# Long convolution and routed experts on one core: the upper frequencies' products on the way out, in two row tiles and two banks

## The chip, the cores and the metric

The kernel runs on one core of a Trainium2 chip. The metric is the time of one execution in microseconds of the device; the median of three runs stands for the kernel. Engines are named as in the profile: PE is TensorE, PEld its weight loads, DVE VectorE, ACT ScalarE, POOL GpSimd, SP SyncE.

## The reference

Two stages follow each other. The first is a long causal convolution of every channel by Fourier transform; the second sends each row of the result to one of 16 experts, a two-layer network of width 1024.

```python
def _attn_ref(x, v, pos_emb, w1, w2):            # x, v: (4, 10048, 128)
    h_mlp = np.maximum(pos_emb @ w1, 0.0) @ w2
    h_filt = h_mlp * np.exp(-0.01 * np.arange(S))[:, None]
    u = x * v
    y = irfft(rfft(u, n=2*S, axis=1) * rfft(h_filt, n=2*S, axis=0)[None], n=2*S, axis=1)[:, :S]
    return x * y

def _moe_ref(x, ...):                            # x: (40192, 128)
    # group by argmax of x @ w_group, expert by argmax of xg @ w_expert[g]
    out[tok] = g_w * e_w * (np.maximum(xg @ w1[g, e], 0.0) @ w2[g, e])
```

## The kernel before

The transform over 20096 positions is split into one over 157 steps of 128 positions and one over the 128 positions inside a step. A channel of one batch is held as 79 frequencies of the outer transform. The first 64 of them (`KM`) lie in `z`, the upper 15 and a row of zeros in `zr`; each frequency has a real and an imaginary part, so that a channel fills 128 rows with its lower frequencies and 32 rows with its upper ones.

The convolution is a loop over the batches. A **pass** of batch b does two things in turns, three channels here and six there: it takes batch b in (`dft_blocks`, L393 on PE, fed by `product` L446 and `fold` L459 on DVE) and it brings batch b-1 out (`turned` and `inverse_blocks`). A **middle** stage follows each pass (`middle`, `back`): products with the filter's spectrum, frequency by frequency. There are four batches, so the way out is done four times: in three passes beside the next batch's way in, and in a last pass that has no batch to take in and that loads the first layer's weights meanwhile. Routing of a finished batch runs along on DVE, and its rows are written out to the experts' pages by indirect transfers that POOL issues (L359). After the convolution the experts' stage (`moe`) runs to the end.

The way out goes by pairs of runs, twelve channels in all (eight in the last pair of a pass). `turned` (L680, L683) transposes on PE, through three buffers of PSUM (`psT`) that ACT copies to `tt` tiles (L685): `tts[0]` holds the upper frequencies, four channels to a tile of 128 rows, and `tts[1]` to `tts[3]` the lower ones, a channel to 128 rows. Then `inverse_blocks` is called for each run of six channels. It issues the load of `x` for the run (`xo`, on ACT's queue, in the last pass on SP's, L696 and L698), takes one of two banks (`psO`, the tile `po`), and writes into it, for each of the two halves of 64 output rows, the products of the upper frequencies (L708) and those of the lower ones (L716):

```python
nc.tensor.matmul(po[hs, c - c0 : c - c0 + m], tts[0][:, g, hs],
                 self.fi[:, h, 1 + c % 4 : 1 + c % 4 + m], start=c == c0, stop=False)      # L708
nc.tensor.matmul(po[hs, c - c0], tts[1 + c // 4][:, c % 4, hs], self.fi[:, h, 0], ...)     # L716
```

A product of L708 contracts over the 128 rows of four channels. Its moving matrix `fi` is block-diagonal, 79 columns for each channel of the run among the four and zeros in the rows of the others; so it has 316 columns where the run has all four channels and 158 where it has two. L716 has 79 columns. The two halves are two column tiles of 64 on PE. ACT then folds the halves into `oo` (L725, L726), DVE adds (`yt`, L731) and multiplies by `xo` (L733); in the last pass POOL does that product for every other run.

The framework puts each instruction at a place on its engine and keeps that order; a tile that is asked for waits until the last reader of the buffer it takes is done. `psO` is also used, some times per batch, by routing's small tiles (`pl`, `pc`, `pe`).

Of the kernel before, what the change touches and what calls it, by code (L numbers as in the profile page):

```python
# [12 lines left out]
F32 = mybir.dt.float32  # L13
# [12 lines left out]
SEQ, D, NB, N1 = 10048, 128, 79, 157  # L26
KM = 64
# [3 lines left out]
NE, G, EG, FF = 16, 4, 4, 1024  # L31
# [7 lines left out]
GI = 6  # L39
# [22 lines left out]
HALVES = slice(0, 64), slice(64, 128)  # L62


def q_of_position():

    q = np.arange(128)
    return np.where(q < 64, 64 + q, 127 - q)


def p_of_position():

    q = np.arange(128)
    return np.where(q < 64, 63 - q, q)


def make_consts():
    f32 = np.float32
    k1 = np.arange(NB)
    ang = 2 * np.pi * ((k1[None, :] * k1[:, None]) % N1) / N1  # L80
    w = (np.where(k1 == 0, 1.0, 2.0) / NN)[:, None]


    fa = np.stack(
        [
            np.stack([np.cos(ang), -np.sin(ang)], 2).reshape(NB, -1),
            np.stack([-np.sin(ang), -np.cos(ang)], 2).reshape(NB, -1),
        ],
        1,
    ).reshape(NB, -1)  # L90


    fi = []
    for swap in range(2):
        both = np.zeros((KM + 16, 2, NB))
        both[:NB, swap] = w * np.cos(ang)
        both[:NB, 1 - swap] = (2 * swap - 1) * w * np.sin(ang)
        rest = np.zeros((4, 32, 4, NB))
        for i in range(4):
            rest[i, :, i] = both[KM:].reshape(32, NB)  # L100
        sign = 1 - 2 * swap
        fi += [sign * both[:KM].reshape(128, -1), sign * rest.reshape(128, -1)]
    fi = np.concatenate(fi, 1)
    k = k1[:, None] + N1 * np.arange(128)[None, :]
    s2 = 2 * np.arange(64) + 1
    a = np.pi * ((k[None] * s2[:, None, None]) % (2 * NN)) / NN
    b = np.concatenate([np.cos(a), np.sin(a)], 0)
    ph = (np.pi * ((k * 127) % (2 * NN)) / NN).T
    phase = np.stack([np.cos(ph), np.sin(ph), -np.cos(ph)], -1)
    win = np.zeros(NR * 128, f32)  # L110
    win[:SEQ] = np.exp(-0.01 * np.arange(SEQ, dtype=f32))
    win = win.reshape(NR, 128)
    return {
        "c_fa": np.concatenate([fa, np.zeros((NR - NB, 4 * NB))]),
        "c_fi": fi,
        "c_b": b,
        "c_bp": np.ascontiguousarray(b.transpose(2, 1, 0)),
        "c_phase": phase.reshape(128, NB * 3),
        "c_win": np.repeat(np.stack([win[:, 64:], win[:, 63::-1]]).transpose(0, 2, 1).reshape(2, -1), 64, 0),
        "c_tri": np.triu(np.ones((128, 128)), 1),  # L120
        "c_id": (np.arange(128)[:, None] * NB + np.arange(NB)[None, :]).astype(f32),
    }
# [10 lines left out]
def groups(n, step):  # L133
    return [(i, min(step, n - i)) for i in range(0, n, step)]


OUTS = groups(120, GI) + [(120, 4), (124, 4)]


class Kernel:  # L140
# [60 lines left out]
    def conv(self, ctx, right):  # L201
        tc, nc, d = self.tc, self.nc, self.d
# [13 lines left out]
        with ExitStack() as c2:  # L216
            self.filter(c2, ahead, made, folded)
        bp = ctx.enter_context(tc.tile_pool(name="back", bufs=1))
        self.fi = bp.tile([128, 2, 5, NB], F32, name="fi")
        nc.sync.dma_start(self.fi.rearrange("p h a t -> p (h a t)"), d["c_fi"])  # L220


# [6 lines left out]
        for b in range(self.nbat + 1):  # L229
            last = b == self.nbat  # L230
            if last:
                ahead.close()
                inner.close()
                self.sp = ctx.enter_context(tc.tile_pool(name="stream", bufs=2, reuse_waits="tile"))
                weights = self.first_weights(right)
                xy = self.z.rearrange("p k s d -> p (k s) d")[:, :NB]
            elif b > 0:
                xy = xyp.tile([128, NB, D], F32, tag="xy", name=f"xy{b - 1}")
            parts = groups(D, GD) if not last else []
            if b == 1:  # L240
                self.router_consts()
            self.run_ahead(b, 0, made, folded)
            for j, (d0, n) in enumerate(OUTS):
                if b > 0 and j % 2 == 0:
                    tts = self.turned(d0, min(2 * GI, D - d0))
                for i in range(2 * j, min(2 * j + 2, len(parts))):
                    self.run_ahead(b, i, made, folded)
                    self.scatter(1 + (i >= 12 and i % 2))
                    self.dft_blocks(*folded[i])
                    if b > 0 and i % 2 == 0:  # L250
                        self.inverse_blocks(b - 1, xy, d0, n, tts)
                if last:
                    self.inverse_blocks(b - 1, xy, d0, n, tts)
                    next(weights, None)
                    if j == 8:
                        self.scatter(sum(1 for s in self.scatters if s[0] < self.nbat - 2))
                        for p in self.all[:XG]:
                            p.load()
                for _ in range(3 if last else 1):
                    next(routing, None)  # L260
                if last:
                    self.scatter(1 + j % 2)
            made, folded = [], []
            if b > 0:
                oh = self.rp.tile([128, NE, NB], F32, tag="oh", name="oh")
                en = self.entries.tile([128, NB, 2], F32, tag="en", name="en")
                routing = chain(self.chosen(b - 1, xy, oh, en), self.ranked(b - 1, oh, en))
                if last:
                    for _ in range(CHOSEN):
                        next(routing)  # L270
            if not last:
                back = []
                for i, (k0, n) in enumerate(groups(NB, 2)):
                    back.append(self.middle(b, k0, n))
                    if len(back) > LAG:
                        self.back(*back.pop(0))
                    if b == 1 and i % 4 == 1:
                        self.clear_rest(i // 4)
                    self.scatter(i % 4 != 3)
                    if i % 4 != 3 if i < 30 else i % 2:  # L280
                        next(routing, None)
                for args in back:
                    self.back(*args)
# [402 lines left out]
            tts.append(tt)  # L686
        return tts

    def inverse_blocks(self, b, xy, d0, n, tts):

        nc, d, sp = self.nc, self.d, self.sp
        rows = lambda t: t[:, : n * NB].rearrange("p (t d) -> p t d", d=n)
# [3 lines left out]
            nc.scalar.dma_start(xo[:, : n * NB], src)  # L696
        else:
            self.tc.keep_in_program_order(nc.sync.dma_start(xo[:, : n * NB], src))  # L698
        po = self.psO.tile([128, GI, NB], F32, tag="po", name="po")
        c0 = d0 % (2 * GI)  # L700

        for c in range(c0, c0 + n):


            if c == c0 or c % 4 == 0:
                g, m = c // 4, min(4 - c % 4, c0 + n - c)
                for h, hs in enumerate(HALVES):
                    nc.tensor.matmul(  # L708
                        po[hs, c - c0 : c - c0 + m].rearrange("p c t -> p (c t)"),
                        tts[0][:, g, hs],  # L710
                        self.fi[:, h, 1 + c % 4 : 1 + c % 4 + m].rearrange("p c t -> p (c t)"),
                        start=c == c0,
                        stop=False,
                    )
            for h, hs in enumerate(HALVES):
                nc.tensor.matmul(  # L716
                    po[hs, c - c0],
                    tts[1 + c // 4][:, c % 4, hs],
                    self.fi[:, h, 0],
                    start=False,  # L720
                    stop=c == c0 + n - 1,
                )
        oo = rows(sp.tile([128, GI * NB], F32, tag="oo", name="oo"))
        by_row = po[:, :n].rearrange("p d t -> p t d")
# [4 lines left out]
        pool, tag, bufs = (self.ap, "y", NY) if b < self.nbat - 1 else (sp, "yt", 2)  # L729
# [639 lines left out]
def layout(x, v, pos_emb, w1, w2, moe_w_group, moe_w_expert, moe_w1, moe_w2):  # L1369

    nbat = x.shape[0]
    c = np.ascontiguousarray

    def blocks(a):
        p = np.zeros((nbat, NR * 128, D), np.float32)
        p[:, :SEQ] = a
        return p.reshape(nbat, NR, 128, D)

    xb, vb = blocks(x), blocks(v)
    q, p = q_of_position(), p_of_position()  # L1380
    pos = np.zeros((NR * 128, 64), np.float32)
    pos[:SEQ] = pos_emb
    pos = pos.reshape(NR, 128, 64)
# [7 lines left out]
    def twice(a):  # L1391
# [4 lines left out]
        "xv_in": c(np.stack([xb[:, :, q], vb[:, :, q]]).transpose(1, 2, 4, 0, 3)),  # L1396
        "x_out": c(
            np.concatenate(
                [xb[:, :NB, p, d0 : d0 + n].transpose(0, 2, 1, 3).reshape(nbat, 128, -1) for d0, n in OUTS], 2
            )  # L1400
        ),
        "pos_t": c(np.stack([pos[:, 64:], pos[:, 63::-1]]).transpose(0, 3, 2, 1).reshape(128, -1)),
# [2 lines left out]
        "w_router": c(  # L1405
            np.concatenate(
                [moe_w_group, moe_w_expert.transpose(1, 0, 2).reshape(128, 16), np.zeros((128, 12), np.float32)], 1
            )
        ),
        "m_w1": c(moe_w1.reshape(NE, 128, FF).transpose(1, 0, 2)),  # L1410
        "m_w2": c(
            moe_w2.reshape(NE, NC, 128, 128).transpose(2, 0, 1, 3).reshape(128, NE, FF)
        ),
# [22 lines left out]
```

## Time and profile before

| | |
|---|---|
| runs of the kernel before | 2050.03, 2047.52, 2046.69 us; median 2047.52 us |
| the profiled execution | 2044.59 us |
| its span | 2042.7 us, mean granted clock 0.977 |
| busy, share of the span | PE 95%, PEld 87%, DVE 79%, ACT 70%, POOL 65% |
| the four times that a batch is brought out | from 250.7, 453.2, 670.0 and 893.8 us on |

The span is measured from the first to the last instruction that the profiler saw; the execution's own time is 1.89 us longer. Busy shares are means over stages with different limits. The end of a matmul is modelled from its size, so PE's busy share is an upper bound; where an engine is at its limit is better read from the distance between starts. A product in 32-bit floats is recorded as two matmuls and two weight loads.

### The profile page before, as it was taken

The numbers are of one execution on the slowest core, as the hardware profiler recorded it, in microseconds if no ns is written. First come the engines' busy times: TensorE is split into PE (matmuls) and PEld (weight loads), VectorE is DVE, ScalarE is ACT, GpSimd is POOL, SyncE is SP. The second block draws the span as 40 slices with busy tenths as digits, with TensorE's granted clock in tenths as the row PEclk, the third lists the DMA queues.
The fourth block names the chain that finished last, engine by engine and source line by source line (L and its number), as shares of the span: only waits on it lengthen the run. The fifth ranks groups of instructions, "written<-read, shape, count | busy, mean of one in ns | idle before, by whom it ended". The sixth has DMA issues, their size and how long they took to land.

```text
span 2042.7 us, 52533 instructions
## 1 busy us (share of the span) xinstructions
PE 1931.5 (95%) x17166; PEld 1778.1 (87%) x17166; DVE 1604.6 (79%) x3462; ACT 1434.3 (70%) x3395; POOL 1320.1 (65%) x1371
## 2 busy tenths in 40 slices
PE   8988999979998799988899999999999999999997
PEld 8867788768876687767799999999999999999997
DVE  6687775796578765894889998889999998888885
ACT  6653387437743575446787888888888888888886
POOL 3157600675799467967176777888888885555554
PEclk9999999989999899999899999999999999999999
DMA  4699966977898588967444544555555544444442
GB/s 138 226 266 262 290 182 194 329 220 205 243 333 262 155 235 283 322 210 261 157 143 127 157 144 149 162 187 165 155 162 157 159 142 135 127 126 131 124 123 66
DMA packets 258715, 388.82 MB, mean 190 GB/s; under 512 B 32680, under 2 KB 132627, under 8 KB 258433
## 3 DMA queue, kind: packets, MB, share of 16 engines
q1 hardware_dynamic: 225024, 318.01, 51.8%
q0 software_dynamic: 23904, 51.83, 7.2%
q10 hardware_dynamic: 9504, 15.54, 2.8%
q8 instruction: 139, 2.28, 0.5%
q14 instruction: 144, 1.17, 0.2%
HBM read 303.24 MB, written 83.04 MB: 189 GB/s over the span
## 4 chain that ended last, share of the span: by engine, by line
PE 50%; POOL 2%; DVE 1%; ACT 1%; DMA 1%; issue 1%; ACTq 0%; DVEq 0%; SPq 0%; POOLq 0%
PE py L1305 8%; PE py L1303 7%; PE py L1304 7%; PE ph L1286 7%; PE ph L1284 7%; PE ph L1285 7%; PE ptm L1317 2%; PE px L1241 2%; POOL wl L1273 1%; POOL out L1329 1%; PE po L708 1%; PE po L716 1%; PE ptr L798 0%; PE pt L683 0%; DMA mw<-m_w 0%
## 5 line engine op out<-in xcount | busy, mean ns | idle before, releaser
L1293 DVE SCALAR_TENSOR_TENSOR hl<-ph,hh 128x512 fp32r<-128x512 f32 x656 | 445.2, 683 | 94.0 <-ACT hh L1292 93.4
L1292 ACT ACTIVATE hh<-ph 128x512 fp32r<-128x512 f32 x656 | 393.8, 600 | 138.7 <-PE ph L1286 70.3
L359 POOL DMA_INDIRECT prow<-stg,adr x316 | 347.1, 1098 | 126.5 <-issue 50.1
L1329 POOL DMA_INDIRECT out<-os,to x328 | 347.9, 1061 | 91.5 <-issue 71.9
L1303 PE MATMUL py<-hh,wh 128*128 128x256 f32 x1312 | 398.5, 304 | 0.0
L1284 PE MATMUL ph<-xh,wh 128*128 128x256 f32 x1312 | 373.3, 285 | 5.1 <-DVE hl L1293 2.6
L1305 PE MATMUL py<-hh,wl 128*128 128x256 f32 x1312 | 373.1, 284 | 5.3 <-POOL wl L1273 5.3
L1286 PE MATMUL ph<-xh,wl 128*128 128x256 f32 x1312 | 373.3, 285 | 0.4 <-DVE wl L1273 0.4
L1285 PE MATMUL ph<-xl,wh 128*128 128x256 f32 x1312 | 372.7, 284 | 0.0
L1304 PE MATMUL py<-hl,wh 128*128 128x256 f32 x1312 | 371.3, 283 | 0.0
L1273 POOL TENSOR_TENSOR wl<-ws,wh 128x512 fp32r<-128x512 f32 x162 | 220.1, 1359 | 201.6 <-ACT wh L1266 200.5
L1305 PEld LDWEIGHTS py<-hh,wl 128*128 128x128 f32 x1312 | 251.2, 192 | 8.2 <-POOL wl L1273 8.1
L1284 PEld LDWEIGHTS ph<-xh,wh 128*128 128x128 f32 x1312 | 252.7, 193 | 5.8 <-ACT hh L1292 2.8
L1286 PEld LDWEIGHTS ph<-xh,wl 128*128 128x128 f32 x1312 | 253.0, 193 | 0.9 <-DVE wl L1273 0.8
L1285 PEld LDWEIGHTS ph<-xl,wh 128*128 128x128 f32 x1312 | 253.0, 193 | 0.1
L1304 PEld LDWEIGHTS py<-hl,wh 128*128 128x128 f32 x1312 | 252.7, 193 | 0.0
L1303 PEld LDWEIGHTS py<-hh,wh 128*128 128x128 f32 x1312 | 251.9, 192 | 0.0
L1273 DVE TENSOR_TENSOR wl<-mw,wh 128x512 fp32r<-128x512 f32 x328 | 238.1, 726 | 0.0
L642 POOL TENSOR_TENSOR y<-t 128x256 f32<-128x256 f32 (+1 forms) x160 | 120.7, 755 | 146.0 <-DVE t L641 141.9
L1266 ACT CAST wh<-mw 128x512 fp32r x328 | 205.7, 628 | 0.0
L1266 ACT CAST wh<-ws 128x512 fp32r<-128x512 f32 x328 | 204.8, 624 | 1.3 <-DMA ws<-m_w 1.3
L393 PE MATMUL psa<-fa,eo 96*64 96x158 f32 x2048 | 182.6, 312 | 13.9 <-POOL eo L464 4.7
(237 smaller groups left out, 4198.0 us busy)
## 6 DMA issues: line engine op xcount, KB each, us to landing
ws<-m_w SPq DMA_DIRECT2D x328, 256.0 KB
ht<-hspec SPq DMA_DIRECT2D x156, 256.0 KB
xv<-xv_in SPq DMA_DIRECT2D x131, 288.0 KB
bt<-c_b SPq DMA_DIRECT2D x95, 256.0 KB
xg<-prow SPq DMA_DIRECT2D x164, 130.0 KB
bp<-c_bp SPq DMA_DIRECT2D x76, 256.0 KB
stg<-xyd SPq DMA_DIRECT2D x76, 256.0 KB
xyd<-xy SPq DMA_DIRECT2D x57, 256.0 KB
```

The lines of the kernel that those rows point to most:

```text
L359: ins = self.nc.gpsimd.indirect_dma_start(self.d["prow"], bass.IndirectOffsetOnAxis(ap=u.adr[:, t : t + 1], axis=0), u.rows[:, t - u.t0], ...
L1266: k.fix(k.nc.scalar.copy(hi, self.matrix(i, half, self.ea)))
L1273: ins = v.tensor_tensor(lo, self.matrix(i, half, self.ed), self.wh[i][half].bitcast(F32), ALU.subtract)
L1284: k.fix(nc.tensor.matmul(ph[:, j], wh, self.xh, start=True, stop=False))
L1285: k.fix(nc.tensor.matmul(ph[:, j], wh, self.xl, start=False, stop=False))
L1286: k.fix(nc.tensor.matmul(ph[:, j], wl, self.xh, start=False, stop=True))
L1292: k.fix(nc.scalar.activation(hh, ph, AF.Relu))
L1293: k.fix(nc.vector.scalar_tensor_tensor(hl, ph, 0.0, hh.bitcast(F32), ALU.max, ALU.subtract))
L1303: k.fix(nc.tensor.matmul(self.py, wh, self.hh[c], start=(c == 0), stop=False))
L1304: k.fix(nc.tensor.matmul(self.py, wh, self.hl[c], start=False, stop=False))
L1305: k.fix(nc.tensor.matmul(self.py, wl, self.hh[c], start=False, stop=(c == NC - 1)))
L1329: ins = k.nc.gpsimd.indirect_dma_start(k.d["out"], bass.IndirectOffsetOnAxis(ap=self.to[:, h : h + 1], axis=0), o[:, h], None, bounds_chec ...
```

## The change

The products of the upper frequencies are taken out of `inverse_blocks` into `inverse_rest`, which runs once for each pair of runs, ahead of the first of them, and takes both banks at once. Each set of four channels is cut into two row tiles of 64 rows, that is of two channels. A row tile's products go to a bank of their own, 158 columns each. So the first run's bank holds the first two channels of every four, the second run's the last two. The lower frequencies' products keep their size; they follow in `inverse_blocks`, which takes the bank that `inverse_rest` began. The output's channels now come in that order, and the host puts the channels of `x`, of the router's weights and of the first layer's rows in the same order. `fi` has three blocks of 79 columns for each half in place of five, and is loaded once. No load, copy or addition on another engine is added or taken away.

```diff
@@ make_consts
-        rest = np.zeros((4, 32, 4, NB))
+        rest = np.zeros((4, 32, 2, NB))
         for i in range(4):
-            rest[i, :, i] = both[KM:].reshape(32, NB)
+            rest[i, :, i % 2] = both[KM:].reshape(32, NB)
@@
+def channels():
+    order = []
+    for i, (d0, n) in enumerate(OUTS):
+        first = d0 - i % 2 * n
+        order += [first + 4 * (c // 2) + i % 2 * 2 + c % 2 for c in range(n)]
+    return np.array(order)
@@ conv
-        self.fi = bp.tile([128, 2, 5, NB], F32, name="fi")
+        self.fi = bp.tile([128, 2, 3, NB], F32, name="fi")
@@
                     if b > 0 and i % 2 == 0:
-                        self.inverse_blocks(b - 1, xy, d0, n, tts)
+                        if j % 2 == 0:
+                            pos = self.inverse_rest(min(2 * GI, D - d0), tts)
+                        self.inverse_blocks(b - 1, xy, d0, n, tts, pos[j % 2], j % 2)
                 if last:
-                    self.inverse_blocks(b - 1, xy, d0, n, tts)
+                    if j % 2 == 0:
+                        pos = self.inverse_rest(min(2 * GI, D - d0), tts)
+                    self.inverse_blocks(b - 1, xy, d0, n, tts, pos[j % 2], j % 2)
@@
-    def inverse_blocks(self, b, xy, d0, n, tts):
+    def inverse_rest(self, n, tts):
+        pos = [self.psO.tile([128, GI, NB], F32, tag="po", name="po") for _ in range(2)]
+        for g in range(n // 4):
+            for h, hs in enumerate(HALVES):
+                for po, rs in zip(pos, HALVES):
+                    self.nc.tensor.matmul(
+                        po[hs, 2 * g : 2 * g + 2].rearrange("p c t -> p (c t)"),
+                        tts[0][rs, g, hs],
+                        self.fi[rs, h, 1:3].rearrange("p c t -> p (c t)"),
+                        start=g == 0,
+                        stop=False,
+                    )
+        return pos
+
+    def inverse_blocks(self, b, xy, d0, n, tts, po, run):
@@
-        po = self.psO.tile([128, GI, NB], F32, tag="po", name="po")
-        c0 = d0 % (2 * GI)
-        for c in range(c0, c0 + n):
-            if c == c0 or c % 4 == 0:
-                g, m = c // 4, min(4 - c % 4, c0 + n - c)
-                for h, hs in enumerate(HALVES):
-                    nc.tensor.matmul(
-                        po[hs, c - c0 : c - c0 + m].rearrange("p c t -> p (c t)"),
-                        tts[0][:, g, hs],
-                        self.fi[:, h, 1 + c % 4 : 1 + c % 4 + m].rearrange("p c t -> p (c t)"),
-                        start=c == c0,
-                        stop=False,
-                    )
+        for c in range(n):
             for h, hs in enumerate(HALVES):
                 nc.tensor.matmul(
-                    po[hs, c - c0],
-                    tts[1 + c // 4][:, c % 4, hs],
+                    po[hs, c],
+                    tts[1 + c // 2][:, 2 * run + c % 2, hs],
                     self.fi[:, h, 0],
                     start=False,
-                    stop=c == c0 + n - 1,
+                    stop=c == n - 1,
                 )
@@ layout
-                [xb[:, :NB, p, d0 : d0 + n].transpose(0, 2, 1, 3).reshape(nbat, 128, -1) for d0, n in OUTS], 2
+                [xb[:, :NB, p][..., chan[d0 : d0 + n]].transpose(0, 2, 1, 3).reshape(nbat, 128, -1) for d0, n in OUTS], 2
...
-            )
+            )[chan]
-        "m_w1": c(moe_w1.reshape(NE, 128, FF).transpose(1, 0, 2)),
+        "m_w1": c(moe_w1.reshape(NE, 128, FF)[:, chan].transpose(1, 0, 2)),
```

## Rows read from the trace of the kernel before

**Rows 1.** Stretches of ten pairs each, pass by pass: length, busy by engine, clock, DMA share, GB/s.
```profile
core 0: us, PE busy (x) PEld busy (x) DVE busy (x) ACT busy (x) POOL busy (x), PEclk, DMA share, GB/s
250.70:342.40 91.70, 90.58 (x1260) 80.94 (x1260) 61.30 (x114) 75.60 (x196) 0.00 (x0) 1.00 0.65 181
453.20:555.80 102.60, 94.93 (x1266) 84.48 (x1265) 67.77 (x152) 76.71 (x196) 63.58 (x68) 0.97 0.77 218
670.00:785.90 115.90, 104.57 (x1275) 90.79 (x1275) 76.35 (x177) 77.19 (x197) 67.65 (x70) 0.89 0.70 195
893.75:957.40 63.65, 61.15 (x794) 51.54 (x794) 41.50 (x100) 41.99 (x78) 39.17 (x39) 0.97 0.86 291
```

**Rows 2.** Timeline of PE, one pair of the first pass: start, length, what.
```profile
268.52 0.55 PE L680 MATMUL pt<-ident,zr 128*128 128x128 f32 x3
...
271.06 1.02 PE L393 MATMUL psa<-fa,eo 96*64 96x158 f32 x12
271.92 0.70 PE L708 MATMUL po<-fi,tt 128*64 128x316 f32 x4
272.45 0.72 PE L716 MATMUL po<-fi,tt 128*64 128x79 f32 x16
273.00 0.44 PE L708 MATMUL po<-fi,tt 128*64 128x158 f32 x4
273.27 0.45 PE L716 MATMUL po<-fi,tt 128*64 128x79 f32 x8
273.54 1.78 PE L393 MATMUL psa<-fa,eo 96*64 96x158 f32 x24
...
276.78 0.99 PE L393 MATMUL psa<-fa,eo 96*64 96x158 f32 x12
277.70 0.55 PE L680 MATMUL pt<-ident,zr 128*128 128x128 f32 x3
```

**Rows 3.** Timeline of PE, one pair of the last pass.
```profile
951.41 0.55 PE L680 MATMUL pt<-ident,zr 128*128 128x128 f32 x3
...
954.01 0.75 PE L708 MATMUL po<-fi,tt 128*64 128x316 f32 x4
954.60 0.72 PE L716 MATMUL po<-fi,tt 128*64 128x79 f32 x16
955.14 0.45 PE L708 MATMUL po<-fi,tt 128*64 128x158 f32 x4
...
956.76 0.73 PE L716 MATMUL po<-fi,tt 128*64 128x79 f32 x16
957.42 0.44 PE L680 MATMUL pt<-ident,zr 128*128 128x128 f32 x2
```

**Rows 4.** Timeline of PE: the router's products in four column tiles of 32.
```profile
969.07 0.42 PE L806 MATMUL plt<-xrt,wr 128*32 128x128 f32 x8
```

**Rows 5.** One pair of the first and of the last pass, columns as in rows 1.
```profile
268.50:277.70 9.20, 9.16 (x129) 8.13 (x128) 6.51 (x12) 7.71 (x21) 0.00 (x0) 1.00 0.66 183
945.38:951.40 6.02, 5.92 (x82) 5.04 (x79) 2.94 (x4) 4.27 (x8) 5.23 (x7) 1.00 0.89 307
```

**Rows 6.** Waits in the second, third and last pass (453:560, 670:786, 893:962): total, times, longest.
```profile
PE pt L683 <- ACT tt L685: 7.5, 7, 1.9
...
PE pt L683 <- ACT tt L685: 7.5, 5, 2.2
...
DVE yt L731 <- POOL z L733: 6.7, 2, 3.9
```

**Rows 7.** Timeline, first pass: addition of a second run; the next pair's L708 starts at 271.92.
```profile
269.71 0.64 DVE L731 TENSOR_TENSOR yt<-po,oo 128x474 f32<-128x474 f32 x1
```

**Rows 8.** Timeline, last pass: additions of second runs, and the next pair's first product.
```profile
936.88 0.65 DVE L731 TENSOR_TENSOR yt<-po,oo 128x474 f32<-128x474 f32 x1 [3.86 <-POOL z L733]
...
941.93 0.65 DVE L731 TENSOR_TENSOR yt<-po,oo 128x474 f32<-128x474 f32 x1 [2.88 <-POOL z L733]
...
941.97 0.75 PE L708 MATMUL po<-fi,tt 128*64 128x316 f32 x4
```

**Rows 9.** The tile `fi`: its one load, and the stretch that the load falls in.
```profile
L220 SPq DMA_DIRECT2D fi<-c_fi x1: 346/346/346, 126.4 to 126.4; - x1
...
100.00:150.00 50.00, 41.89 (x357) 32.76 (x355) 41.08 (x97) 29.71 (x99) 23.95 (x35) 0.97 1.03 270
```

More of the change, by code (lines that the diff above doesn't have):

```diff
@@ L1379, in layout @@
     xb, vb = blocks(x), blocks(v)
-    q, p = q_of_position(), p_of_position()
+    q, p, chan = q_of_position(), p_of_position(), channels()
     pos = np.zeros((NR * 128, 64), np.float32)
```

## The prediction

> **What bounds the kernel now.** I first asked where the changed instructions lie. They lie only in the four passes that bring a batch out, so I read those as four stretches of ten pairs each, from one pair's first transpose to the eleventh's [rows 1]. The reader is to see two things there: PE is nearly always busy, but a pair takes 9.17 us in the first pass (91.70 / 10), 10.26 in the second, 11.59 in the third and 6.37 in the last (63.65 / 10). The first three do the same work on PE, so the first pass is near PE's own limit, and the second and third lose 1.1 and 2.4 us per pair to other things.
>
> Since the end of a matmul is modelled, I then took the timelines of single pairs and measured from start to start. A pair of the first pass runs without a visible hole: transposes, three channels in, a run out, twice three channels in, and so on, 9.18 us from 268.52 to 277.70 [rows 2]. A pair of the last pass has transposes for 2.60 us (951.41 to 954.01) and 3.41 us of products [rows 3]. In the first pass ACT is busy 7.71 us of 9.20 and DVE 6.51; in the last POOL is busy 5.23 us of 6.02 and the DMA engines 0.89 [rows 5]. These are the limits that lie next behind PE. Last I read the waits, for what the two slow passes lose: the fourth group of transposes waits for ACT's copies, 7.5 us in all in each of those two passes, and in the last pass an addition on DVE waits twice, 6.7 us, for POOL's product [rows 6].
>
> **The upper products before.** From start to start, four records of 316 columns take 272.45 - 271.92 = 0.53 us, four of 158 take 273.27 - 273.00 = 0.27 us; a pair has two of each, so 1.60 us. The lower products take 273.00 - 272.45 = 0.55 us for four channels, and 273.54 - 273.27 = 0.27 us for two [rows 2]; they stay as they are, 1.64 us per pair.
>
> **The upper products after.** Three sets of four channels, each with four products of 158 columns (two halves by two row tiles), each recorded twice: 24 records in place of 16. No row-tiled product stands in this trace, so the price is bounded from both sides. *Below:* if the four tiles run at once, a set takes what four records of 158 columns take now on two tiles, 0.27 us, and a pair 0.81 us. *Above:* if only two run at once, a set takes twice that, 0.54, and a pair 1.62 us. (That the tiles run one after the other, which would be 3.2 us, I exclude: column tiles run in pairs in every row of that kind.) The nearest row is the router's: eight records on four column tiles of 32, each 128 columns wide, are over in 0.42 us [rows 4]. If such a product takes 128/158 of the 0.27 us that a pair of 158-column products takes, that is 0.22 us for two tiles at once; two such rounds would be 0.44 us of starts and an end behind them, while the row ends within 0.42 us with the last product's end in it. So four tiles did run at once there, and each seemed to proceed on its own. I take the lower end: 0.81 us, a saving of 0.79 us per pair of twelve. The pair of eight falls from 2 x 0.53 = 1.06 to 2 x 0.27 = 0.54 us.
>
> The Trainium skill says the same of row tiles: TensorE: Matmul & The Clock Gate, Part 3, gives 3.07 times the speed for four row tiles that run together. Half of it for two, an estimate from that page, would make a pair's upper products 1.60 / 1.53 = 1.05 us, a saving of 0.55. No run here shows it yet.
>
> **The switch of tiling.** The rows of one tile change from 128 to 64 ahead of the upper products and back behind them. What a change of tiling costs can be read at the end of a pair of the last pass: the last sixteen products of L716 start at 956.76, the transposes on the whole array at 957.42, that is 0.66 us, where sixteen take 955.14 - 954.60 = 0.54 when products of the same tiling follow [rows 3]. So 0.12 us here; taking the switch from the way in to the transposes, 277.70 - 276.78 = 0.92 us where 271.92 - 271.06 = 0.86 is usual [rows 2], it would be less, so I take 0.1 us with bounds 0 (if tiles of the same columns need no pause) and 0.12. In the first three passes two switches are added per pair (from the way in, whose 64-column tiles run straight into L708 now, and to L716), in the last one (transposes end in a switch already).
>
> This is also the rule that speaks against the change: TensorEngine Tiling (Array Packing), Key Properties, has TensorE drain when the tiling mode changes. The trace agrees in the direction, by the 0.12 us above [rows 3]; without any drain the sum at PE, below, would be 7.7 us larger.
>
> **Sum at PE.** First three passes: 0.79 - 0.20 = 0.59 us per pair; with the pair of eight (0.52 - 0.20 = 0.32) 10 x 0.59 + 0.32 = 6.2 us per pass. Last pass: 10 x 0.69 + 0.42 = 7.3 us. In all 25.9 us if every pair were bound by PE alone.
>
> **What of it reaches the end.** *First pass:* a pair would fall to 8.6 us, with ACT busy 7.7 of it, in its program's order; ACT's copies free the transposes' buffers, so some of the gain becomes a wait for it. I take three quarters, 4.7 us (bounds 2 and 6.2). *Second pass:* pairs take 1.1 us more than PE needs; half, 3.1 us (0 to 6). *Third:* 2.4 us more than PE needs and a clock of 0.89 [rows 1]; a third, 2 us (-1 to 5). *Last:* POOL's 5.2 us per pair nearly fill the 5.3 us that would be left, and the DMA engines are at 0.86 [rows 1, 5]; a fifth, 1.5 us (-3 to 6), with the next point in it. What is late next is therefore ACT's copies in the first three passes, POOL's product and the loads behind it in the last.
>
> **Both banks at once.** Before, a pair's first product needed only the bank that the first run had left long ago. Now the upper products wait until the second run of the pair before has been added on DVE. Queued behind them on PE are both runs and the next way in; ACT, DVE and then POOL wait for these. In the first pass that addition ends at 269.71 + 0.64 = 270.35 and the next pair's products start at 271.92: 1.57 us to spare, the work that covers it being transposes and three channels in [rows 7]. In the last pass only transposes lie between, and where the addition has waited for POOL it ends at 942.58, after 941.97 where the products start now: 0.6 us of new wait in that pair [rows 8]. Three to five such pairs cost 2 to 3 us; it is in my figure for the last pass.
>
> **Edits at no cost.** `fi` shrinks from 3160 to 1896 bytes per partition, 0.16 MB less; its load falls in a stretch where the DMA engines are full at 270 GB/s, so at most 0.6 us [rows 9], and nothing if the load is not what the stretch waits for; I take 0. The order of channels changes no size of any load, copy or addition. The lower products of the first run now read all three `tts` of a pair, but the upper ones give ACT 0.8 us to finish the last. No transfer is issued in the moved step.
>
> **Sum.** 4.7 + 3.1 + 2.0 + 1.5 = 11.3 us. Against the profiled execution, 2044.59 us, that gives 2033.3; the median of the runs lies 2.9 us above the profiled one, so the forecast is 2047.5 - 11.3, rounded to 2036 us. The runs of before spread over 3.3 us; 0.2%, 4.1 us, is about what a measurement can tell from no change.
>
> **Rivals.**
>
> *A. The row tiles do not run at once (slower).* The place is L708's successor, the price: saving 1.60 - 1.62, about 0, and the switches remain, 3 x 11 x 0.2 + 11 x 0.1 = 7.7 us, plus 2 us of waits for the bank: 2057 us; 2050 if the switches are hidden in the passes that wait for others. For it: no row-tiled product here. Against it: column tiles do run four at once [rows 4], and the two row tiles write to different banks. It decides when a set takes over 0.47 us, since from there 0.2 us of switches eat the saving.
>
> *B. The gain goes into waits (no change).* PE's pairs get shorter, but ACT in the first pass, DVE and routing in the second and third, POOL and transfers in the last take up all but 3 us: 2044 us. For it: the two slow passes [rows 1] and the waits for ACT [rows 6]. Against it: the first pass, with PE without a hole [rows 2].
>
> *C. Waits for the second bank decide (slower).* With the tiles at once, but 1.5 us of wait in each of ten pairs of the last pass and 1 us in each of the twenty of the two slow ones: 35 us against 26, so 2057 us; it tips at a mean wait of about 0.6 us per pair. For it: rows 8 of this very wait in the making; against it: 1.57 us to spare in the first pass [rows 7].
>
> *D. PE is bound everywhere (more).* All 25.9 us arrive: 2022 us. Against it stand the waits [rows 6].
>
> **Chances.** Forecast, a gain of 5 to 22 us: 0.59. B: 0.17. A: 0.16, of which a quarter hidden well enough to be no change. C: 0.06. D: 0.02. Faster by over 0.2%: 0.59 + 0.02 = 0.61; within: 0.17 + 0.04 = 0.21; slower: 0.12 + 0.06 = 0.18. The range runs from 2025 (a gain of 22, nearly the whole sum) to 2051 (A at its mild end), which leaves out D, most of C and the harder half of A. The forecast's own range is 2025 to 2042.
>
> **What would show it.** Right: the upper products as 24 records of 158 columns on 64 rows, a set every 0.27 us, 0.8 us per pair; ten pairs of the first pass in about 87 us, and the last pass little shorter than 63.65. Wrong at the first step: a set every 0.53 us. Wrong at the switch: more than 0.12 us between the upper products and those around them. Wrong at the bank: waits of PE's upper products for DVE's addition of more than 0.5 us per pair outside the last pass. It would also be wrong if the passes got shorter and the middle stages or the experts' stage longer by as much; I see no term for that.

## The result and the profile after

The changed kernel takes 2065.98 us (median of 4 runs, 2064.99 to 2069.34) where the kernel before takes 2047.47 beside it: 1.0091 times as long, 95% interval 1.0074 to 1.0109. The forecast was 2036 us, the range 2025 to 2051. The change made the kernel 18.5 us slower; measured again (e9 below) it took 1.0069 times as long (1.0045 to 1.0093). The profiled execution took 2065.51 us, with a span of 2063.6 us.

The same stretches of ten pairs as in [rows 1], read from the windows of the kernel after, with the same columns:

```profile
252.09:352.47 100.38, 87.14 (x1342) 77.34 (x1342) 62.03 (x114) 78.35 (x196) 0.00 (x0) 0.98 0.61 164
463.18:573.41 110.23, 92.41 (x1346) 80.53 (x1346) 70.18 (x151) 79.07 (x196) 63.13 (x66) 0.92 0.72 201
691.18:803.80 112.62, 99.23 (x1356) 84.89 (x1356) 77.43 (x177) 78.11 (x197) 67.58 (x68) 0.89 0.70 200
912.36:977.09 64.73, 58.32 (x876) 50.68 (x876) 38.73 (x98) 42.13 (x78) 41.37 (x41) 0.96 0.86 289
```

PE is busy less in every pass (87.14 us against 90.58 in the first), as it was meant to be, and yet the first pass grew by 8.68 us and the second by 7.63; the third shrank by 3.28 and the last grew by 1.08. The starts and ends of these rows and of [rows 1] give what lies between: the stretches from pass to pass changed by -0.09, +3.57 and +0.71 us, the way to the first pass by +1.39 and the way from the last to the end by +1.2. The nine sum to the 20.9 us by which the spans differ (2063.6 - 2042.7). The first two passes hold 16.3 us of it, the stretch between the second and the third pass 3.6.

The timeline of PE in the first pass after, to be held against [rows 2]:

```profile
263.66 0.85 PE L696 MATMUL pt<-ident,z 128*128 128x128 f32 x4 [2.23 <-ACT tt L698]
...
265.40 1.04 PE L708 MATMUL po<-fi,tt 64*64 64x158 f32 x24
266.37 1.04 PE L729 MATMUL po<-fi,tt 128*64 128x79 f32 x24
...
273.34 0.85 PE L696 MATMUL pt<-ident,z 128*128 128x128 f32 x4 [1.04 <-ACT tt L698]
...
283.88 0.85 PE L696 MATMUL pt<-ident,z 128*128 128x128 f32 x4 [1.90 <-ACT tt L698]
```

Two things are to be seen. The upper products (L708) are 24 records on 64 rows, and from their start to that of the lower ones (L729) they take 266.37 - 265.40 = 0.97 us, where they took 1.60. But the last transposes of a pair, which used to follow the others almost at once (waits of 0.8 us in all in the whole first pass, below), now wait 1.0 to 2.2 us, in the pairs shown, for ACT's copies of the earlier ones. A pair takes 273.34 - 263.66 = 9.68 and then 283.88 - 273.34 = 10.54 us; it took 9.18.

So the question is why ACT is late. The waits of the first pass (253:342), total, times, longest; first the kernel before, then the one after:

```profile
DVE xv L446 <- DMA xv<-xv_in: 20.2, 23, 1.5
...
PE pt L683 <- ACT tt L685: 0.8, 2, 0.5
ACT xv L457 <- DVE xv L446: 0.8, 1, 0.8
```

```profile
DVE xv L459 <- DMA xv<-xv_in: 28.5, 31, 3.0
ACT xv L470 <- DVE xv L459: 17.5, 21, 1.8
...
PE pt L696 <- ACT tt L698: 11.5, 7, 2.2
```

They make a chain: DVE's product waits for a load of x, ACT's negation waits for that product (0.8 us before, 17.5 now), and ACT's copies, which PE's transposes need, stand behind the negation in ACT's queue. At its head is the load. That it is late because of the order of DVE's instructions is what the timelines suggest; the experiments below test it. In a pair DVE does four products (xv, first step of a channel group on the way in), four folds (eo, the last reader of the loaded tile, which frees its buffer for the next load), two additions (yt) and two products on the way out (xy). Timeline of DVE before, one pair (its first addition is in [rows 7]):

```profile
269.23 0.55 DVE L446 TENSOR_TENSOR xv<-xv 96x384 f32<-96x384 f32 x1 [1.15 <-DMA xv<-xv_in]
...
270.27 0.55 DVE L459 TENSOR_TENSOR eo<-xv 96x384 f32<-96x384 f32 x1
270.74 0.65 DVE L733 TENSOR_TENSOR xy<-yt,xo 128x474 f32<-128x474 f32 x1
271.40 0.55 DVE L446 TENSOR_TENSOR xv<-xv 96x384 f32<-96x384 f32 x1
272.13 0.55 DVE L459 TENSOR_TENSOR eo<-xv 96x384 f32<-96x384 f32 x1 [0.18 <-PE psa L393]
274.08 0.56 DVE L446 TENSOR_TENSOR xv<-xv 96x384 f32<-96x384 f32 x1 [1.40 <-DMA xv<-xv_in]
274.63 0.56 DVE L459 TENSOR_TENSOR eo<-xv 96x384 f32<-96x384 f32 x1
275.11 0.64 DVE L731 TENSOR_TENSOR yt<-po,oo 128x474 f32<-128x474 f32 x1
275.67 0.54 DVE L459 TENSOR_TENSOR eo<-xv 96x384 f32<-96x384 f32 x1
276.14 0.64 DVE L733 TENSOR_TENSOR xy<-yt,xo 128x474 f32<-128x474 f32 x1
276.88 0.55 DVE L446 TENSOR_TENSOR xv<-xv 96x384 f32<-96x384 f32 x1
```

And after, one whole pair and the start of the next:

```profile
269.51 0.55 DVE L459 TENSOR_TENSOR xv<-xv 96x384 f32<-96x384 f32 x1 [2.97 <-DMA xv<-xv_in]
269.98 0.64 DVE L744 TENSOR_TENSOR yt<-po,oo 128x474 f32<-128x474 f32 x1
270.55 0.55 DVE L472 TENSOR_TENSOR eo<-xv 96x384 f32<-96x384 f32 x1
271.01 0.64 DVE L746 TENSOR_TENSOR xy<-yt,xo 128x474 f32<-128x474 f32 x1
271.57 1.02 DVE L472 TENSOR_TENSOR eo<-xv 96x384 f32<-96x384 f32 x2
272.51 0.64 DVE L744 TENSOR_TENSOR yt<-po,oo 128x474 f32<-128x474 f32 x1
273.19 0.65 DVE L746 TENSOR_TENSOR xy<-yt,xo 128x474 f32<-128x474 f32 x1
274.07 0.55 DVE L459 TENSOR_TENSOR xv<-xv 96x384 f32<-96x384 f32 x1 [0.23 <-DMA xv<-xv_in]
275.19 0.55 DVE L472 TENSOR_TENSOR eo<-xv 96x384 f32<-96x384 f32 x1 [0.57 <-PE psa L406]
276.38 0.56 DVE L459 TENSOR_TENSOR xv<-xv 96x384 f32<-96x384 f32 x1 [0.63 <-DMA xv<-xv_in]
277.46 0.56 DVE L459 TENSOR_TENSOR xv<-xv 96x384 f32<-96x384 f32 x1 [0.52 <-DMA xv<-xv_in]
280.12 0.56 DVE L459 TENSOR_TENSOR xv<-xv 96x384 f32<-96x384 f32 x1 [2.11 <-DMA xv<-xv_in]
```

With P a product, F a fold, Y an addition and X a product on the way out, a pair was P Y F X P F P F Y F X P and is P Y F X F F Y X P F P P. Three folds now lie within 2.04 us (270.55 to 272.59), then comes one at 275.19 and no other up to 280.12, so three of the five load buffers come free in a bunch and their loads run together. The loads' own starts in the two traces (SP's queue) show that each is issued within 0.1 us of a fold's end: before at 270.88, 272.76, 275.22, 276.29 and 279.90 us, after at 271.15, 272.18, 272.65, 275.81 and 281.78. The DMA line of the two traces shows it (262:285, GB/s in 40 slices, before and then after):

```profile
GB/s 43 144 305 70 145 281 382 81 83 176 267 155 220 322 197 67 0 123 294 136 177 350 314 55 117 169 235 171 220 341 198 26 48 150 333 60 208 373 265 31
```

```profile
GB/s 144 192 241 123 269 139 0 30 158 343 343 259 211 13 0 14 0 112 171 246 96 150 369 279 198 301 186 298 180 264 65 10 0 0 0 0 134 315 144 171
```

Slices under 50 GB/s: five before, eleven after, and those eleven in three gaps. No line of the change puts DVE's instructions in another order; the order is worked out by the framework from the program, and moving the upper products to the head of a pair was enough for it to come out differently (ACT's too; on PE, in the first two passes, the groups other than the upper products kept their order, and only single records at their seams changed places).

### The profile page after: what moved, and what is told of

It reads as the page before. It is cut to its first block, busy times and chain, and to the rows that moved or that the text cites. A ratio compares the mean times of both kernels' runs of the same rounds, so it can differ in the third digit from the quotient of the medians.

```text
span 2063.6 us, 53237 instructions
## 1 busy us (share of the span) xinstructions
PE 1919.7 (93%) x17518; PEld 1764.7 (86%) x17518; DVE 1604.0 (78%) x3462; ACT 1441.7 (70%) x3395; POOL 1320.7 (64%) x1371
## 4 chain that ended last, share of the span: by engine, by line
PE 66%; DMA 8%; DVE 8%; POOL 5%; issue 4%; ACT 4%; SPq 1%; ACTq 0%; DVEq 0%; POOLq 0%
PE py L1318 7%; PE ph L1299 7%; PE ph L1297 7%; PE py L1316 7%; PE py L1317 7%; PE ph L1298 7%; PE psb L488 6%; DMA xv<-xv_in 5%; PE pbp L670 4%; PE psa L406 2%; PE ptm L1330 2%; PE px L1254 2%; PE ptr L811 2%; PE plt L819 1%; PE pt L696 1%
## 5 line engine op out<-in xcount | busy, mean ns | idle before, releaser
L670 PE MATMUL pbp<-y,bp 128*128 128x256 f32 x632 | 169.7, 394 | 26.2 <-POOL y L658 25.6
```

## The experiments

*Theory O (order):* regrouping the products made DVE and ACT work in another order; this starves the loads and costs more than the tiles save. *Theory B (banks):* the loss is that a pair's upper products need both banks. *Theory T (tiles):* the tiles or the switches cost more than was saved. The order is varied by pinning: each product, fold, addition and copy of the first three passes of DVE (and ACT) is held behind the one ahead of it in an order taken from the other kernel; nothing else is changed.

On the chips of the first eight and of the four runs e13 to e16 the kernel before itself took 2115 to 2119 us, so of these runs I read the ratio and the first pass, which is as long there as elsewhere. Later passes and whole times are compared among e9 to e12 (one chip), e17 and e18 (another), where before took 2048 to 2049 us; what these show of the sixth buffer does not hold on the other chips, as said below.

**e1, e16: regrouped, without row tiles** (128-row products on block-diagonal constants, as before the change).

```
...
-                        tts[0][rs, g, hs],
-                        self.fi[rs, h, 1:3].rearrange("p c t -> p (c t)"),
+                        tts[0][:, g, hs],
+                        self.fi[:, h, 1 + 2 * r : 3 + 2 * r].rearrange("p c t -> p (c t)"),
...
```

> The changed kernel with its upper products regrouped in the same way (ahead of both runs, into both banks), but each contracting over all 128 rows against a block-diagonal matrix, as before; the orders on DVE and ACT come out the same as in the changed kernel. Theory 'order' (the framework's new order of DVE's and ACT's instructions in the passes costs the time, the row tiles save some): still slow, ten pairs of the first pass 99 to 106 us, 2064 to 2082 us in all. Rival 'tiling' (the row tiles or the switches of tiling cost the time): back near the kernel before, 91 to 94 us, 2045 to 2053 us. Rival 'banks' (taking both banks at once costs the time): slow as under 'order'.

> The regrouped products over all 128 rows, for the whole time; same order as the changed kernel. 'Order': 1.006 to 1.016, first pass 99 to 102 us: the row tiles neither cost nor save where the passes wait for the loads. If the row tiles cost: 1.000 to 1.004.

Ratios 1.008 (1.0039 to 1.0122) and 1.0100 (1.0062 to 1.0138), first pass 100.7 and 99.2 us. DVE's order was that of the changed kernel. The loss is there without a single row tile, and in e16 at a granted clock of 1.00 through the first pass: T falls as its cause, and in that pass the clock is not the cause either. e16 also gives the price of the upper products when only two tiles run at once, the same 24 records on 128 rows (timeline of PE, 268:290):

```profile
273.49 1.84 PE L708 MATMUL po<-fi,tt 128*64 128x158 f32 x24
275.12 1.04 PE L729 MATMUL po<-fi,tt 128*64 128x79 f32 x24
```

From start to start that is 1.63 us, against 0.97 with row tiles.

**e2, e5, e13, e18: the changed kernel in the order of before; e4: DVE's order alone.**

```
...
+        for order in ORDERS:
+            at, last = {k: iter(v) for k, v in self.seen.items()}, None
+            for kind in order:
+                ins = next(at[kind])
+                if last is not None:
+                    self.after(ins, last)
+                last = ins
...
```

> The changed kernel, with the passes' additions, products and copies on DVE and ACT pinned to the order that they had in the kernel before. 'Order': the loss is gone and the row tiles show, ten pairs of the first pass 85 to 89 us, 2027 to 2043 us. 'Banks': no change against the changed kernel, 98 to 102 us, 2060 to 2070 us. 'Tiling': the same, 2058 to 2070 us.

> The changed kernel with the order of before on DVE and ACT, once more, since the runs beside it had spread over 40 us. 'Order' and 'loads' (the order costs the time; the row tiles save PE time, but the five load buffers hold the passes near their old length): ten pairs of the first pass 91 to 94 us, in all 2043 to 2058 us. 'Order' alone (nothing else bounds): 85 to 89 us and 2027 to 2043. If the order is not the cause: 2060 to 2070 us.

> The changed kernel with DVE alone pinned to the order of before; ACT's order is the framework's. 'Order', if DVE's bunched products and folds (and so the freeing of the load buffers) are what costs: as the run with both pinned, 85 to 90 us for ten pairs, 2027 to 2045 us. If it is ACT's order (negations ahead of the copies that PE waits for): 95 to 101 us, 2055 to 2068 us.

> The changed kernel with the order of before on DVE and ACT and its five load buffers, for the whole time, which the two earlier runs of it could not give beside a kernel before that spread over 40 us. 'Order': the loss is gone, 0.992 to 1.001 of the kernel before, first pass 91 to 95 us. If the order matters in the first pass alone: 1.000 to 1.005.

> The changed kernel with the order of before and five load buffers, likewise. 'Order' as the whole of the loss: 0.990 to 1.001 of the kernel before; 1.003 to 1.006 if the last pass and the middle stages keep a part of the loss.

Ratios 1.0029 (0.9978 to 1.0079), 1.0048 (0.9999 to 1.0098), 1.0021 (0.9982 to 1.0059) and, the closest, e18's 1.0026 (1.001 to 1.0042); first passes 92.9, 95.4, 92.7 and 94.6 us. e4: 1.0041 (0.999 to 1.0092), 93.1 us. The old order gives most of the first pass's loss back, and DVE's alone does (e4). But the 85 to 90 us that 'Order' forecast for e2 and e4 did not come, and not even in the old order is the kernel faster than before; the waits of e18 in the stretch 264:342 say why:

```profile
DVE xv L497 <- DMA xv<-xv_in: 25.6, 15, 2.9
...
PE pt L738 <- ACT tt L740: 6.9, 8, 1.6
```

DVE still waits 25.6 us for loads, where the kernel before waits 17.4 in that stretch. So O explains only part: with a shorter pair on PE, five buffers do not bring loads in time in the old order either. In the second pass e18 takes 106.7 us, where the changed kernel takes 110.2 (111.6 in e9) and the kernel before 102.6: there the old order gives back about half. The third takes 113.9 us in e18 and 114.1 in e9, so it does not depend on the order.

**e3, e6, e14: the kernel before in the order of the changed one** (the same edit, the other way round).

> The kernel before, with the same instructions pinned to the order that they have in the changed kernel; its matmuls are untouched. 'Order': slow, ten pairs of the first pass 97 to 105 us, 2062 to 2080 us. 'Banks' and 'tiling': as before, 91 to 93 us, 2045 to 2051 us.

> The kernel before with the changed kernel's order on DVE and ACT, once more for the same reason. 'Order': ten pairs of the first pass 99 to 104 us, in all 2060 to 2080 us. If the matmuls or the banks are the cause: 91 to 93 us and 2045 to 2052 us.

> The kernel before with the changed kernel's order, for the whole time. 'Order': 1.007 to 1.014 of the kernel before, first pass 99 to 104 us. If regrouping the products, with both banks, costs by itself: 1.000 to 1.006.

Ratios 1.0049 (1.0007 to 1.0092), 1.0059 (1.0019 to 1.0098), 1.0068 (1.0037 to 1.0099); first passes 101.8, 103.2 and 103.1 us, for 91.7. The matmuls, tiles and banks of before lose 10 to 11.5 us in the first pass when only the order is the new one; for the whole time e14 lies just under the 1.007 to 1.014 that 'Order' gave it. The waits of e14 (264:342) are of the kind and nearly of the size of the changed kernel's, which in the same stretch are 24.1, 15.0 and 11.5 us:

```profile
DVE xv L484 <- DMA xv<-xv_in: 28.2, 28, 3.0
ACT xv L498 <- DVE xv L484: 16.9, 20, 1.4
...
PE pt L725 <- ACT tt L727: 7.2, 6, 1.8
```

This settles O for the first pass.

**e7, e11: old order and a sixth load buffer; e8, e15, e17: the same for the kernel before; e10: sixth buffer, new order.** If the five buffers bind, a sixth must free the row tiles' gain. Its space is taken from the `yt` buffers.

```
-NLOAD, NPROD, NSPEC, NTT, NY = 5, 5, 4, 5, 5
+NLOAD, NPROD, NSPEC, NTT, NY = 6, 5, 4, 5, 4
```

> The changed kernel with the order of before and six load buffers in place of five (and four y buffers in place of five, for the room). 'Loads': with a sixth buffer DVE's waits for the loads go from some 25 us to under 10 in the first pass and ten pairs take 84 to 88 us. Rival 'ACT' (ACT's 7.7 us per pair, in its order, holds the pass): ten pairs stay at 90 to 94 us.

> The kernel before, its order pinned to its own, with the same buffers (six load, four y). 'Loads': PE bounds the first pass here, so ten pairs stay at 90 to 92 us although the waits for loads fall. If loads bounded the kernel before as well: 84 to 88 us.

> The kernel before, in its own order, with six load and four y buffers. It splits the 1.2% of the run with row tiles and six loads: if the loads alone give it, 0.986 to 0.991; if the row tiles give what PE saves (0.4 us per pair, some 14 us with the last pass), 0.993 to 0.997; first pass 91 to 92 us either way.

> The changed kernel as it is, beside the kernel before and the next three on one chip, since the chips of the earlier runs took 2119 us for the kernel before in place of 2047. Ten pairs of the first pass 99 to 102 us; a ratio of 1.006 to 1.012 to the kernel before.

> The changed kernel, pinned to its own order on DVE and ACT, with six load buffers (and four y buffers). If the new order costs because its three products and three folds in a row empty and fill the five load buffers by bunches ('ring'): most of the loss is gone, 87 to 92 us for ten pairs of the first pass. If the order costs by itself (negations ahead of the copies on ACT, whatever the loads do): 96 to 102 us.

> The changed kernel with the order of before and six load buffers, in more rounds and beside the others: 87 to 89 us for ten pairs of the first pass; 1.0 to 2.0% faster than the changed kernel as it is, and 0.994 to 1.001 of the kernel before.

> The kernel before with six load and four y buffers, in its own order, once more, for a chip on which the kernel before takes 2047 us. If the loads alone give the 1.2% that row tiles, old order and six loads gave together there: 0.985 to 0.991, with the second and third pass shorter and the first at 91 to 92 us. If row tiles and loads share it: 0.992 to 0.997. If the sixth buffer helps only the faster matmuls: 0.998 to 1.002.

| kernel | ratio to before | us | first pass, us |
|---|---|---|---|
| e7 rows, old order, six | 0.9971 (0.992 to 1.0023) | | 87.7 |
| e8, e15 before, six | 1.0022 (0.9982 to 1.0063), 1.0005 (0.9979 to 1.0031) | | 91.7, 91.6 |
| e9 changed, unaltered | 1.0069 (1.0045 to 1.0093) | 2063.26 | 100.0 |
| e10 rows, new order, six | 0.9952 (0.9936 to 0.9967) | 2037.76 | 90.4 |
| e11 rows, old order, six | 0.9882 (0.9857 to 0.9908) | 2023.95 | 87.7 |
| e17 before, six | 0.9915 (0.9897 to 0.9933) | 2032.13 | 91.7 |

Windows as in [rows 1], of e11:

```profile
251.97:339.63 87.66, 86.25 (x1345) 76.46 (x1345) 59.14 (x114) 76.22 (x196) 0.00 (x0) 1.00 0.68 187
449.49:544.36 94.87, 88.96 (x1345) 78.23 (x1346) 70.11 (x155) 76.77 (x196) 64.76 (x66) 0.98 0.86 237
...
873.44:936.80 63.36, 57.41 (x875) 49.85 (x876) 39.06 (x99) 42.03 (x78) 38.99 (x39) 0.97 0.85 292
```

And of e17:

```profile
250.96:342.61 91.65, 90.75 (x1264) 81.21 (x1264) 59.58 (x114) 75.81 (x196) 0.00 (x0) 1.00 0.65 180
453.70:551.39 97.69, 93.59 (x1266) 83.59 (x1264) 69.03 (x155) 75.42 (x195) 66.50 (x68) 0.98 0.84 233
```

In the first pass of e11 PE is busy again without a hole to speak of (86.25 of 87.66), and DVE waits for PE instead of for loads; the first row of its waits (264:334):

```profile
DVE eo L513 <- PE psa L442: 19.9, 16, 1.8
```

The sixth buffer alone does nothing for before's first pass (91.65; 91.70 in [rows 1]), where PE is the limit, but takes 4.9 us from its second. On the chip of e17 it is worth 0.85% by itself (1 - 0.9915), and row tiles in the old order 0.33% more (0.9882 / 0.9915 = 0.9967, between two chips, a gain that its interval, about 0.3% either way, barely tells from none). On the chips where before takes 2115 to 2119 us it is worth nothing that the runs can tell (e8 and e15), and e11's kernel, run there as e7, comes out at 0.9971, with no clear gain: DVE's waits for loads are gone from the second pass of e8 too, but the pass still takes 115.5 us, with PE waiting 11.2 us for ACT's copies (455:568). Why those chips are slower there is open. e15 fitted neither branch of its expectation, e17 lies between two, and e11 beat its own (0.994 to 1.001). The new order still costs 0.7% with six buffers (0.9952 / 0.9882), though loads are no longer what it waits for in the first pass, which is 2.7 us longer than e11's. Its second pass takes 103.2 us for e11's 94.9, on the same chip and with nothing but the order changed, so the order costs 8.3 us there (at a mean granted clock of 0.95 for 0.98, which no run separates from the waits).

**e12: e11 without the row tiles and the common start in the last pass**, where each run again takes only its own bank.

```
...
-                    self.inverse_blocks(b - 1, xy, d0, n, tts, pos[j % 2], j % 2)
+                    self.inverse_blocks(b - 1, xy, d0, n, tts, None, j % 2)
...
+            if own and c % 2 == 0:
+                for h, hs in enumerate(HALVES):
+                    nc.tensor.matmul(
+                        po[hs, c : c + 2].rearrange("p c t -> p (c t)"),
+                        tts[0][:, c // 2, hs],
+                        self.fi[:, h, 1 + 2 * run : 3 + 2 * run].rearrange("p c t -> p (c t)"),
...
```

> As the run beside it (order of before, six load buffers), with row tiles and both banks in the first three passes alone; in the last pass each run takes its own bank and contracts over all 128 rows, as before. If taking both banks at once costs time in the last pass: 1 to 6 us less than the run beside it, 0.990 to 0.999 of the kernel before. If the last pass gains by row tiles: 1 to 3 us more than the run beside it.

2023.82 us, 0.9884 (0.9863 to 0.9905), against e11's 0.9882; the last pass 62.5 against 63.4 us. Neither branch of the expectation came: the whole time is the same, and the last pass 0.9 us shorter. Since e12 takes away the row tiles there as well, their gain and the wait for the bank may cancel; it does not separate them. Against theory B stand other runs: e14 loses in the first pass with the banks as before, and e11, which takes both banks at once in every pass, has no loss at all. The wait itself exists, in the last pass of the changed kernel (timeline of PE):

```profile
953.30 0.48 PE L708 MATMUL po<-fi,tt 64*64 64x158 f32 x2
955.47 1.85 PE L708 MATMUL po<-fi,tt 64*64 64x158 f32 x22 [1.69 <-DVE yt L744]
```

It comes four times, 3.7 us in all (912:977). e11 and e12, at 2024 us, are the best versions, 1.2% faster than before on their chip; the same kernel as e11 came to 0.9971 on e7's.

## Why the prediction was wrong

- **The step that failed** is "What of it reaches the end", in its first two figures (4.7 us in the first pass with bounds 2 and 6.2, 3.1 in the second with 0 to 6), where the passes grew by 8.7 and 7.6. Its ground was that PE bounds the first pass and that ACT's copies are next. I took the order of DVE's and ACT's instructions as given, and never asked whether moving the upper products might change it; nor did I give a term to DVE's waits for loads, which stood in the trace of before with 20.2 us in the first pass. They cost nothing while PE was the limit, and yet the five load buffers were the next limit, closer than ACT's 7.71 us of 9.20: in the old order the shorter pair still takes 94.6 us for ten with five buffers (e18) and 87.7 with six (e11). That the order makes the loss is shown by e3, e6 and e14 (alone it costs 10 to 11.5 us in the first pass), by e10 against e11 (8.3 us in the second) and by e1 and e16 (the same loss without row tiles).
- **"The order of channels changes no size", "No transfer is issued in the moved step"** were right as far as they went. The loads moved all the same, since they are issued when a fold frees a buffer, and the folds moved.
- **The upper products** run four at once, as taken: rival A is wrong. Three sets take 0.97 us with the switches in it, against a lower bound of 0.81 and an upper of 1.62 without; e16's 24 records on 128 rows, two tiles at once, take 1.63. The Trainium skill's page TensorE: Matmul & The Clock Gate, Part 3, has matmuls on different row groups run concurrently. The trace agrees, by the 0.97 us against 1.63.
- **The switch of tiling was mis-sized.** Where PE is the limit, the pair fell from 9.20 us in e17 to 8.80 in e11, so by 0.4, not 0.59. The parts can be read in e11: the three channels in, ahead of the upper products, take 289.83 - 288.88 = 0.95 us (0.86 before), the upper ones 290.80 - 289.83 = 0.97 (three sets of 0.27 would be 0.81), the six lower ones behind them 291.67 - 290.80 = 0.87 (0.82 before). That is 0.30 us for the two switches where 0.20 was put, an estimate, since it takes the products themselves at 0.81. The other 0.1 us is in the transposes, which with the wait of 0.16 for ACT's copies in the first row below take 288.88 - 286.22 = 2.66 us, for 289.72 - 287.14 = 2.58 in e17. So a switch costs 0.15 us on the mean, above my upper bound of 0.12. The Trainium skill's page TensorEngine Tiling (Array Packing), Key Properties, has TensorE drain when the tiling mode changes; these rows agree that a change costs time, and do not show how.

```profile
288.10 0.85 PE L738 MATMUL pt<-ident,z 128*128 128x128 f32 x4 [0.16 <-ACT tt L740]
288.88 1.03 PE L442 MATMUL psa<-fa,eo 96*64 96x158 f32 x12
289.83 1.04 PE L750 MATMUL po<-fi,tt 64*64 64x158 f32 x24
290.80 1.04 PE L771 MATMUL po<-fi,tt 128*64 128x79 f32 x24
291.67 1.78 PE L442 MATMUL psa<-fa,eo 96*64 96x158 f32 x24
```

- **The first pass's term would have held** with order and loads out of the way: e11 is 91.65 - 87.66 = 4.0 us shorter than e17, for 4.7 predicted. The whole sum would have been too high even so: the medians of e17 and e11, on two chips, differ by 8.2 us, for 11.3.
- **Both banks at once** (2 to 3 us in the last pass) was right in place and nearly in size: four waits, 3.7 us, and none in the first pass. The last pass's term was not: 1.1 us lost for 1.5 gained. Rival C names a wait that does not decide: e11 has both banks at once and is faster than the kernel before.
- **Rival B** came nearest: the gain did go into waits, and waits for ACT at that. But it made the loss at most as large as the gain; it had no reason why a wait should grow past what PE saved.

**The 18.5 us.** The new order with five buffers is 0.43% by e9 and e18 (1.0069 against 1.0026, on two chips), some 9 us, 0.65% if the result's own 1.0091 is taken, and 0.68% by e14, where nothing but the order differs from the kernel before; the 0.26% that remain in e18 go when the sixth buffer comes. The rest of the picture is open: how the framework comes to the other order; why the third pass got shorter (115.90 to 112.62 us) and does so in either order; the 3.57 us between the second and the third pass; and what the new order waits for in e10 beyond the 12.5 us in which DVE's additions wait for ACT (264:334).

## What to carry to other kernels

Before costing a saving on the engine that bounds a stage, read who waits for what on the others: a ring of buffers whose loads already come late can be the next limit, as here, even while its waits cost nothing. Where a framework orders the instructions, a regrouping on one engine is a change to all of them: compare the order on each engine, and pin the old one, before judging the idea. Here the order cost more than the idea saved, and on two of the chips one more load buffer was worth more than the idea.

## What the runs showed of the hardware

- Products on 64 rows by 64 columns ran four at once, in f32 and into two banks: 24 records of 158 columns took 0.97 us, a part of the two switches included, and the same 24 on 128 rows 1.63 us (e16).
- A switch between 128 and 64 rows cost about 0.15 us (an estimate: half of the 0.30 us that e11's rows give for the way there and back) in the middle of a run of products, more than the 0.12 us of the one at the end of a pair in the last pass [rows 3].
- Chips differ by 3% in this kernel: 2047 to 2049 us on some, 2115 to 2119 on others, while ten pairs of the first pass take as long on both (e8 and e15 against e17: 91.7, 91.6 and 91.7 us).
